# Key sums on TensorE instead of GpSimd in the first two batches of a fused attention and mixture-of-depths kernel

## The chip, the cores and the metric

The kernel runs on one core of one Trainium2 chip. TensorE (PE in the profile, with PEld for its weight loads), VectorE (DVE), ScalarE (ACT), GpSimd (POOL) and the DMA queues, issued mostly from SyncE (SP), run beside each other and are ordered by semaphores. The metric is the device time of one execution in microseconds; the time shown for the kernel before is the median of three runs.

## What is computed

Attention with RMS-normalised queries and keys, and on its output a mixture of depths: in each batch the 128 tokens with the highest score go through two layers with a residual, the other tokens are left as they are.

```python
# q, k, v: (8 batches, 12 heads, 448 tokens, 64), float32
q_n = q / sqrt(mean(q * q, -1) + 1e-6) * g_q
k_n = k / sqrt(mean(k * k, -1) + 1e-6) * g_k
p = exp(q_n @ k_n.T / 8)                      # scores, softmax
x = (p @ v) / sum(p over keys)                # (8, 448, 768)
s = x @ w_gate
top = the 128 tokens of each batch with the largest s
out = x
out[top] = x[top] + sigmoid(s[top]) * (relu(x[top] @ w1) @ w2)   # 768 -> 1024 -> 768
```

The change touches the line with `sum(p over keys)`: how the denominators are added up, and when some of the work around them is issued.

## The kernel before

**Tiling.** Four heads of one batch form a group `n`; there are 24 groups, three to a batch. The 448 keys of a group are seven tiles of 64, and one key tile of a group is a unit `u`. `scores(u)` (L292) makes four matmuls of 64x64 tiles, and ScalarE's exp (L301) turns them into a tile `p` of 128 partitions (two heads of 64 keys) by 2 x 448 queries. The ring of `p` tiles holds seven. `values(u)` (L316) multiplies `p` with `v` and accumulates a group's seven units in PSUM.

**Denominators.** `add_probs(u)` decides what becomes of a `p` tile. Normally VectorE adds the seven tiles into `sum` (L338). In the first six groups (two batches; `by_pool`) GpSimd adds tiles 0 and 1 into a buffer that once held input tokens (L332), VectorE adds tiles 2 to 5 (three additions) and then the tile of GpSimd (L342), and tile 6 goes to TensorE as it is (`sums_last`). The last group also leaves tile 6 to TensorE. `sum_keys(n)` (L372) adds over the partitions: it multiplies each term (`sum`, and a left over `p`) with `pick_pair`, a pattern of ones of 128 x 32, in four column tiles of TensorE, 224 query columns each, into the PSUM tile `den_ps`. ScalarE copies the result (L380). `invert_sums(n)` transposes it twice (L397, `denT_ps`) and takes the reciprocal on VectorE (L399, `rden`). `to_tokens(n, c)` transposes the attention output (L415, `x_ps`) and multiplies it with `rden` (L417) to give `x`.

**Gate and layers.** When a group is done, `gate(n)` (L441) multiplies `x` with the gate weights. When a batch is done, `spread` (L454), `score_rows` (L470), `count` (L486), `annotate` and `select` rank its tokens and write the chosen ones to DRAM with indirect DMAs from GpSimd (L513); `load_selected` (L531) loads them as `xe`. `mixture(g)` is a generator over the layers of a set of batches: batch 0 alone, then pairs, then single ones. It transposes `xe` (L561), runs the first layer (L590) and the second (L609, L618) and stores rows (L628). It yields after each half bank of work; what lies between two yields is called a piece.

**Order of the work.** The order is written out by a loop over sections `q` of four units in two halves. Each half issues the scores of two units and, one pair behind, the values; then `opening` takes at most one due task (`sum_keys`, `invert_sums`, `to_tokens`, `last_tokens`, `score_rows`), `run(slots)` issues what stands in the list `todo` for these two slots (loads, squares L210 and L219, the power on GpSimd L220, scaling of queries L251, gates, counts), and `piece(q)` advances the layers by one piece. `ready` holds the section from which a set of batches may begin its layers. `before_layers(q)` is true until batch 0's layers have begun; until then a bank of PSUM of their pool, `moe`, serves `denT_ps` and `x_ps`. `begin` covers the sections up to three batches' units and some more; in these, and around the third and fourth piece of a pair of batches (`slow`), the second half gets no piece. `long_next(q)` says whether the second half has a piece, in which case `invert_sums` comes right behind it in the same section.

Of the kernel before, what the change touches and what calls it, by code (L numbers as in the profile page):

```python
# [10 lines left out]
F32 = mybir.dt.float32  # L11
I32 = mybir.dt.int32
AF = mybir.ActivationFunctionType
OP = mybir.AluOpType
# [11 lines left out]
class Loads:  # L26
# [37 lines left out]
    def get(self, name, n, i=None):  # L64
        return self.tiles[name, n, i]
# [3 lines left out]
def fast(  # L69
# [21 lines left out]
    nc = tc.nc  # L91

    B, NP, _, S = loads.src["qT"].shape
    CP = 112
    NJ = S // CP
    D = 64
    NI = S // D
    H = 2 * NP
    GH = 4
    NG = H // GH  # L100
# [7 lines left out]
    n_groups = B * NG  # L108
    scale = 1.0 / math.sqrt(D)

    const = ctx.enter_context(tc.tile_pool(name="const", bufs=1))
    norm_pool = ctx.enter_context(tc.tile_pool(name="norm", bufs=2))
# [14 lines left out]
    def aux(shape, name):  # L127

        if PER * now[0] >= units:
            return ps_sc.tile(shape, F32, tag="sc", name=name)  # L130
        if spare[0]:
            return ps_moe.tile(shape, F32, tag="moe", name=name)
        return ps_aux.tile(shape, F32, tag="aux", name=name)
# [7 lines left out]
    load, get, neg_half = loads.load, loads.get, loads.neg_half  # L141

    ident = const.tile([128, 128], F32, name="ident")
# [10 lines left out]

    gg = const.tile([128, 1], F32, name="gg")

    pick_pair = const.tile([128, 32], F32, name="pick_pair")
    nc.vector.memset(pick_pair, 0.0)
    for c in range(2):
        nc.vector.memset(pick_pair[D * c : D * (c + 1), c : c + 1], 1.0)  # L160
    nc.vector.scalar_tensor_tensor(
        out=gg, in0=loads.gcol[:, 0:1], scalar=scale, in1=loads.gcol[:, 1:2], op0=OP.mult, op1=OP.mult
    )

    ps = ps_moe.tile([128, 512], F32, tag="moe", name="warm_ps")
# [116 lines left out]
    probs, sums, avs, xTs, rdens, xs = {}, {}, {}, {}, {}, {}  # L282
# [40 lines left out]

    def add_probs(u):
        n, i = divmod(u, NI)
        if i == NI - 1 and sums_last(n):
            lasts.setdefault(n, []).append(probs.pop(u))
            return
        first = 2 if by_pool(n) else 0
        if first and i == 1:  # L330
            t = first_tokens[n % 2].rearrange("p h i d -> p h (i d)")
            nc.gpsimd.tensor_tensor(out=t, in0=probs.pop(u - 1), in1=probs.pop(u), op=OP.add)  # L332
            firsts[n] = t
        elif i > first:
            begins = i == first + 1
            if begins:
                sums[n] = p_pool.tile([128, 2, S], F32, name="sum", bufs=2)
            nc.vector.tensor_tensor(  # L338
                out=sums[n], in0=probs.pop(u - 1) if begins else sums[n], in1=probs.pop(u), op=OP.add
            )  # L340
            if first and i == NI - 2:
                nc.vector.tensor_tensor(out=sums[n], in0=sums[n], in1=firsts.pop(n), op=OP.add)  # L342

    def values_out(n):
        for c in (1, 0):
# [2 lines left out]
            xTs[n, c] = t  # L348
        avs.pop(n)

    dens, lasts, firsts = {}, {}, {}

    first_tokens = [get("tok", 0, i) for i in range(2)]

    def sums_last(n):


        return n < 2 * NG or n == n_groups - 1

    def by_pool(n):  # L360

        return n < 2 * NG

    def sum_keys(n):

        ps = aux([128, 512], "den_ps")
        terms = [sums.pop(n)] + lasts.pop(n, [])
        for t in terms:
            for hh in range(2):
                for odd in range(2):  # L370
                    o = 64 * odd + 32 * hh
                    nc.tensor.matmul(  # L372
                        out=ps[o : o + 32, 0 : S // 2],
                        lhsT=pick_pair,
                        rhs=t[:, hh].rearrange("k (jj odd p) -> k odd jj p", odd=2, p=CP)[:, odd],
                        start=(t is terms[0]),
                        stop=(t is terms[-1]),
                    )
        den = norm_pool.tile([128, NJ // 2, CP], F32, name="den", bufs=1)
        nc.scalar.copy(out=den.rearrange("d j p -> d (j p)"), in_=ps[:, 0 : S // 2])  # L380
        dens[n] = den
        if n < n_groups - 1:

            q, place = now
            when = (q, place + 1) if place == 0 or long_next(q) else (q + 1, 0)
            tasks.insert(0, (when, lambda: invert_sums(n)))

    def invert_sums(n):
        den = dens.pop(n)
        shape = [128, NJ // 2, 128]  # L390
        if now[1] == 0 and PER * now[0] < units:
            pool, tag = (ps_moe, "moe") if before_layers(now[0]) else (ps_sc, "sc")
            ps = pool.tile(shape, F32, tag=tag, name="denT_ps")
        else:
            ps = aux(shape, "denT_ps")
        for jj in range(NJ // 2):
            nc.tensor.transpose(out=ps[:CP, jj, :], in_=den[:, jj, :], identity=ident)  # L397
        rden = norm_pool.tile([CP, NJ // 2, 4, 2], F32, name="rden")
        nc.vector.reciprocal(  # L399
            out=rden, in_=ps[:CP].rearrange("p jj (t r) -> p jj t r", r=32)[:, :, :, 0:2]  # L400
        )
        rdens[n] = rden.rearrange("p jj (odd hh) c -> p (jj odd) hh c", hh=2)

    def to_tokens(n, c):
        b = n // NG
        if b not in xs:
            xs[b] = x_pool.tile([CP, NJ, DX], F32, name="x")
        t = xTs.pop((n, c))
        shape = [128, NJ, 128]
        if c == 1 and not before_layers(now[0]):  # L410
            ps = ps_sc.tile(shape, F32, tag="sc", name="x_ps")
        else:
            ps = aux(shape, "x_ps")
        for j in range(NJ):
            nc.tensor.transpose(out=ps[:CP, j, :], in_=t[:, j, :], identity=ident)  # L415
        col = (n % NG * 2 + c) * 128
        nc.vector.tensor_tensor(  # L417
            out=xs[b][:, :, col : col + 128].rearrange("p j (h d) -> p j h d", d=D),
            in0=ps[:CP].rearrange("p j (h d) -> p j h d", d=D),
            in1=rdens[n][:, :, :, c, None].to_broadcast([CP, NJ, 2, D]),  # L420
            op=OP.mult,
        )
# [113 lines left out]
    group_of = {b: g for g, bs in enumerate(groups) for b in bs}  # L536
# [100 lines left out]

    HALVES = 2
    PER = 2 * HALVES
    BEGIN = 3 * NG * NI // PER + 5  # L640
    units = n_groups * NI
    todo, tasks = {}, []

    def at(slot, fn, *args):
        todo.setdefault(slot, []).append(lambda: fn(*args))
# [31 lines left out]
    for n in range(1, n_groups):  # L677
# [4 lines left out]
        if n > 1:  # L682
# [3 lines left out]
            first = max(s0 - (20 if n > 5 else 17), 0)  # L686
# [17 lines left out]

    def long_next(q):

        if before_layers(q) or q in begin:
            return False
        return 2 <= pieces[0] < pieces[1]

    def before_layers(q):
        return done == 0 and ready.get(0, q + 1) > q

    def soon():

        q, place = now
        return PER * q + 2 * place if PER * q < units else -9

    def last_tokens(n):
        to_tokens(n, 1)  # L720
        b, g = divmod(n, NG)
        s = soon()
        at(s, gate, n)
        if g < NG - 1:
            return

        at(s + 4 if s >= 0 else s, store_x, b)
        at(s + 1, spread, b)
        q, place = now

        when = (q + 1 + place // 2, 0) if b < B - 1 else (q + 1, 1)
        tasks.insert(0, (when, lambda: ranks_of(b)))

    def ranks_of(b):
        score_rows(b)
        s = soon()
        at(s, count, b, (0, 1))
        at(s + 1, count, b, (2, 3))
        at(s + 2, annotate, b)
        at(s + 2, select, b)  # L740
        at(s + 10 if s >= 0 else s + 3, load_selected, b)
        if b == B - 1:
            ready[group_of[b]] = 0
        elif b == groups[group_of[b]][-1]:
            ready[group_of[b]] = (s + 8) // PER + 1

    def run_values(upto, q):
        ended = False
# [25 lines left out]
    def short(q):  # L774

        return pieces[0] == 1

    def piece(q):

        nonlocal moe, done  # L780
        slow = range(3, 5) if q * PER < units and pieces[1] > 10 else ()
        if half == 1 and (q in begin and pieces[0] > 2 or pieces[0] in slow):
            return False
        pieces[0] += 1
        if next(moe, moe) is not moe:
            return True
        if ready.get(done, q + 1) > q:
            return False
        moe = mixture(done)
        pieces[:] = 1, 2 + 8 * len(groups[done])  # L790
        done += 1
        next(moe)
        return True


    begin = range(BEGIN)
    pieces = [0, 0]
    waiting = list(range(units))
    moe, ready, done, q = iter(()), {}, 0, 0
    while done < len(groups) or tasks:  # L800
        now[:] = q, 0
        k = PER * q
# [552 lines left out]
```

## Time and profile before

| | |
|---|---|
| median of three runs | 522.48 us (521.94 to 523.08) |
| profiled execution | 523.67 us |
| its span | 521.9 us |
| TensorE clock granted | 0.999 |
| TensorE busy | 96% of the span, 4133 matmuls and transposes |
| VectorE, ScalarE, GpSimd busy | 65%, 53%, 38% |
| DMA | 93.17 MB, mean 179 GB/s |

The profile comes from one execution, and its times are those of that execution. Its span runs from the first to the last instruction. Busy time is time in which an engine had an instruction; that says nothing yet of the path that sets the end. A group of instructions is listed by its line, engine, operation, output<-inputs and shapes, with its busy time, the mean duration of one instruction and the idle time of the engine ahead of it, with what ended the idle time. Durations of matmuls overlap, since their ends are modelled; the distance from start to start tells what one costs.

### The profile page before, as it was taken

How to read it: one execution, taken by the hardware profiler on the slowest of the kernel's cores; microseconds unless marked ns; L12 is line 12 of the kernel's file. 1: busy time of each engine (PE TensorE's matmuls, PEld its weight loads, DVE VectorE, ACT ScalarE, POOL GpSimd, SP SyncE). 2: the span in 40 equal slices, each digit the busy share in tenths (PEclk: the TensorE clock that was granted, in tenths of full speed). 3: DMA queues.
4: the chain of work that ended last, by engine and by line, in shares of the span. 5: the costliest groups of instructions: out<-in, count | busy, mean ns of one | idle time of the engine just before them, and what ended most of it. 6: DMA issues, size and time to landing. Idle time of an engine off the chain costs nothing. (4 is left out here: it accounts for less than half of the span.)

```text
span 521.9 us, 10414 instructions
## 1 busy us (share of the span) xinstructions
PE 499.3 (96%) x4133; PEld 283.1 (54%) x4133; DVE 338.0 (65%) x636; ACT 277.0 (53%) x507; POOL 198.1 (38%) x110
## 2 busy tenths in 40 slices
PE   5999898899999999999999999999999999899996
PEld 4544343365754534556654454556564464686595
DVE  4578798679867799697656775788464675440101
ACT  4887876666657667675454544764643434310010
POOL 4997768433544084435411344036110132020002
PEclk9999999999999999999999999999999999999999
DMA  8978879989864549968167373586222042031001
GB/s 298 374 239 292 292 242 334 313 233 328 274 177 131 153 142 312 261 229 261 26 201 221 107 240 111 187 264 180 80 76 68 4 148 77 1 122 47 30 32 35
DMA packets 43402, 93.17 MB, mean 179 GB/s; under 512 B 11059, under 2 KB 23348, under 8 KB 43346
## 3 DMA queue, kind: packets, MB, share of 16 engines
q1 hardware_dynamic: 39938, 86.11, 52.6%
q0 software_dynamic: 3264, 6.31, 3.4%
q8 instruction: 34, 0.56, 0.5%
q14 instruction: 22, 0.18, 0.1%
q10 hardware_dynamic: 144, 0.00, 0.0%
HBM read 74.93 MB, written 25.35 MB: 192 GB/s over the span
## 5 line engine op out<-in xcount | busy, mean ns | idle before, releaser
L301 ACT ACTIVATE p<-sc,rinv 128x448 f32<-128x448 f32 x336 | 186.5, 642 | 105.4 <-PE sc L292 79.8
L220 POOL TENSOR_TENSOR rinv<-ss,neg_half 128x14 f32<-128x14 f32 (+1 forms) x49 | 131.3, 2685 | 178.0 <-DVE ss L219 144.9
L292 PE MATMUL sc<-qT,kT 64*64 64x448 f32 x1344 | 153.2, 545 | 2.0 <-DVE x L417 1.2
L316 PE MATMUL av<-p,v 64*64 64x448 f32 x1344 | 146.8, 537 | 0.0
L338 DVE TENSOR_TENSOR sum<-sum,p 128x896 f32<-128x896 f32 x101 | 110.1, 1090 | 8.7 <-ACT p L301 2.5
L316 PEld LDWEIGHTS av<-p,v 64*64 64x64 f32 x1344 | 59.4, 133 | 67.7 <-issue 58.0
L292 PEld LDWEIGHTS sc<-qT,kT 64*64 64x64 f32 x1344 | 54.0, 132 | 70.6 <-issue 46.6
L219 DVE TENSOR_REDUCE ss<-sq 128x14 f32<-128x910 f32 (+1 forms) x49 | 52.4, 1074 | 18.7 <-ACT sq L210 18.5
L417 DVE TENSOR_TENSOR x<-x_ps,rden 112x512 f32<-112x512 f32 x48 | 32.9, 689 | 37.9 <-PE x_ps L415 34.6
L513 POOL DMA_INDIRECT selected<-x,rank x32 | 35.4, 1105 | 58.0 <-DVE x L505 50.0
L590 PE MATMUL moe_ps<-xeT,w 128*128 128x256 f32 (+1 forms) x288 | 56.0, 346 | 0.0
L609 PE MATMUL moe_ps<-w,hT 128*128 128x384 f32 x160 | 55.8, 492 | 0.0
L590 PEld LDWEIGHTS moe_ps<-xeT,w 128*128 128x128 f32 x288 | 46.2, 191 | 7.0 <-issue 2.8
L210 ACT ACTIVATE sq<-tok 128x896 f32<-128x896 f32 (+1 forms) x49 | 46.3, 952 | 6.2 <-DMA tok<-in_tok_dram 6.2
L441 DVE SCALAR_TENSOR_TENSOR prod<-x,wg 112x256 f32<-112x256 f32 x96 | 40.7, 424 | 3.1
L628 POOL DMA_INDIRECT out_dram<-xe,row x10 | 11.4, 1136 | 80.7 <-DVE xe L618 63.6
L609 PEld LDWEIGHTS moe_ps<-w,hT 128*128 128x128 f32 x160 | 28.8, 190 | 20.2 <-issue 4.3
L618 DVE SCALAR_TENSOR_TENSOR xe<-sc,xe 128x384 f32<-128x384 f32 (+1 forms) x7 | 3.9, 560 | 48.1 <-PE sc L609 48.1
L590 PE MATMUL sc<-xeT,w 128*128 128x256 f32 (+1 forms) x192 | 32.2, 328 | 0.3 <-ACT xeT L566 0.3
L609 PE MATMUL sc<-w,hT 128*128 128x384 f32 (+1 forms) x112 | 31.3, 440 | 0.0
L415 PE MATMUL x_ps<-ident,xT 128*112 128x128 f32 x192 | 28.9, 276 | 2.2 <-DVE rden L399 2.2
L590 PEld LDWEIGHTS sc<-xeT,w 128*128 128x128 f32 x192 | 28.8, 191 | 2.9 <-ACT xeT L566 0.5
(69 smaller groups left out, 316.2 us busy)
## 6 DMA issues: line engine op xcount, KB each, us to landing
tok<-in_tok_dram SPq DMA_DIRECT2D x48, 448.0 KB
qT<-in_qT_dram SPq DMA_DIRECT2D x24, 448.0 KB
kT<-in_kT_dram SPq DMA_DIRECT2D x24, 448.0 KB
v<-in_vp_dram SPq DMA_DIRECT2D x24, 448.0 KB
out_dram<-x SPq DMA_DIRECT2D x8, 1344.0 KB
bc<-rows SPq DMA_DIRECT2D x44, 224.0 KB
xe<-selected SPq DMA_DIRECT2D x8, 385.0 KB
w<-in_moe_w_dram SPq DMA_DIRECT2D x6, 512.0 KB
```

Of the source, the lines that this page charges most:

```text
L210: nc.scalar.activation(out=sq[:, h, :, 0:D], in_=t[:, h], func=AF.Square, scale=scale)
L219: nc.vector.tensor_reduce(out=ss[:, h], in_=sq[:, h], axis=AX.X, op=OP.add)
L220: nc.gpsimd.tensor_tensor(out=rinv[:, h].rearrange(flat), in0=ss[:, h].rearrange(flat), in1=neg_half.to_broadcast([128, (h.stop - h.start) ...
L292: nc.tensor.matmul(out=scs[hh][D * c : D * (c + 1), 0:S], lhsT=get("kT", n)[r, c, D * i : D * (i + 1)], rhs=get("qT", n)[r, c, :], start=True,
L301: nc.scalar.activation(out=p[:, hh], in_=scs[hh][:, 0:S], func=AF.Exp, scale=rinvs[n, 1][:, hh, i : i + 1],)
L316: nc.tensor.matmul(out=avs[n][c][D * hh : D * (hh + 1), 0:S], lhsT=get("v", n)[r, hh, i, :], rhs=probs[u][r, hh], start=(i == 0), stop=(i ...
L338: nc.vector.tensor_tensor(out=sums[n], in0=probs.pop(u - 1) if begins else sums[n], in1=probs.pop(u), op=OP.add)
L417: nc.vector.tensor_tensor(out=xs[b][:, :, col : col + 128].rearrange("p j (h d) -> p j h d", d=D), in0=ps[:CP].rearrange("p j (h d) -> p j ...
L441: nc.vector.scalar_tensor_tensor(out=prod, in0=xs[b][:, j, cols], scalar=1.0, in1=wg[:, cols], op0=OP.mult, op1=OP.mult, accum_out=gates[b ...
L513: w = nc.gpsimd.indirect_dma_start(out=t[:, :], out_offset=bass.IndirectOffsetOnAxis(ap=rank[:, j : j + 1], axis=0), in_=x[:, j, :], in_of ...
L590: nc.tensor.matmul(out=ps[:, i, :, :n], lhsT=w1[:, dc, 128 * (f0 + i) : 128 * (f0 + i + 1)], rhs=xeT[:, dc, 0:G, :n], start=(dc == 0), sto ...
L609: nc.tensor.matmul(out=ps[:n, :width], lhsT=hT[:, fc, i, :n], rhs=w2[:, fc, cols], start=(fc == 0), stop=(fc == NFC - 1),)
```

## The change

The change has two sides. In `add_probs`, `sum_keys` and `invert_sums` it alters who adds up the denominators:

- GpSimd no longer adds. In the first six groups VectorE adds tiles 0 to 4 (four additions) and tiles 5 and 6 both go to TensorE; the last group keeps one tile for TensorE.
- `pick_pair` holds two patterns of 128 x 32. Each term now takes eight matmuls of 112 columns instead of four of 224: the two values of `jj` are added into the same 112 columns of PSUM, in different rows.
- Accordingly the copy is 128 x 112, there is one transpose instead of two, and the reciprocal writes `rden` through a permuted view.

In the order of the work it alters five places: `BEGIN` is one section later; one function `single(q)` replaces the two tests for sections without a second piece, and is now also asked by `long_next`; batch 0's layers may begin one section later; the gate of group 1 is issued two slots later and that of group 22 four slots later.

```diff
-    pick_pair = const.tile([128, 32], F32, name="pick_pair")
+    pick_pair = const.tile([128, NJ // 2, 32], F32, name="pick_pair")
     nc.vector.memset(pick_pair, 0.0)
-    for c in range(2):
-        nc.vector.memset(pick_pair[D * c : D * (c + 1), c : c + 1], 1.0)
+    for jj in range(NJ // 2):
+        for c in range(2):
+            r = 2 * jj + c
+            nc.vector.memset(pick_pair[D * c : D * (c + 1), jj, r : r + 1], 1.0)
...
     def add_probs(u):
         n, i = divmod(u, NI)
-        if i == NI - 1 and sums_last(n):
+        if i >= NI - by_array(n):
             lasts.setdefault(n, []).append(probs.pop(u))
-            return
-        first = 2 if by_pool(n) else 0
-        if first and i == 1:
-            t = first_tokens[n % 2].rearrange("p h i d -> p h (i d)")
-            nc.gpsimd.tensor_tensor(out=t, in0=probs.pop(u - 1), in1=probs.pop(u), op=OP.add)
-            firsts[n] = t
-        elif i > first:
-            begins = i == first + 1
+        elif i > 0:
+            begins = i == 1
...
-            if first and i == NI - 2:
-                nc.vector.tensor_tensor(out=sums[n], in0=sums[n], in1=firsts.pop(n), op=OP.add)
...
+    def by_array(n):
+
+        return 2 if n < 2 * NG else 1 if n == n_groups - 1 else 0
...
-        for t in terms:
+        steps = [(t, jj) for t in terms for jj in range(NJ // 2)]
+        for step in steps:
+            t, jj = step
             for hh in range(2):
                 for odd in range(2):
                     o = 64 * odd + 32 * hh
                     nc.tensor.matmul(
-                        out=ps[o : o + 32, 0 : S // 2],
-                        lhsT=pick_pair,
-                        rhs=t[:, hh].rearrange("k (jj odd p) -> k odd jj p", odd=2, p=CP)[:, odd],
-                        start=(t is terms[0]),
-                        stop=(t is terms[-1]),
+                        out=ps[o : o + 32, 0:CP],
+                        lhsT=pick_pair[:, jj],
+                        rhs=t[:, hh].rearrange("k (j p) -> k j p", p=CP)[:, 2 * jj + odd],
+                        start=(step is steps[0]),
+                        stop=(step is steps[-1]),
                     )
-        den = norm_pool.tile([128, NJ // 2, CP], F32, name="den", bufs=1)
-        nc.scalar.copy(out=den.rearrange("d j p -> d (j p)"), in_=ps[:, 0 : S // 2])
+        den = norm_pool.tile([128, CP], F32, name="den", bufs=1)
+        nc.scalar.copy(out=den, in_=ps[:, 0:CP])
...
-        for jj in range(NJ // 2):
-            nc.tensor.transpose(out=ps[:CP, jj, :], in_=den[:, jj, :], identity=ident)
-        rden = norm_pool.tile([CP, NJ // 2, 4, 2], F32, name="rden")
+        nc.tensor.transpose(out=ps[:CP, :], in_=den, identity=ident)
+        rden = norm_pool.tile([CP, NJ // 2, 2, 2, 2], F32, name="rden")
...
-    BEGIN = 3 * NG * NI // PER + 5
+    BEGIN = 3 * NG * NI // PER + 6
...
-        if before_layers(q) or q in begin:
+        if before_layers(q) or single(q):
             return False
         return 2 <= pieces[0] < pieces[1]
...
-        at(s, gate, n)
+        at(s + (2 if n == 1 else 4 if n == n_groups - 2 else 0), gate, n)
...
-            ready[group_of[b]] = (s + 8) // PER + 1
+            ready[group_of[b]] = (s + 8) // PER + (1 if b else 2)
...
+    def single(q):
+
+        if q in begin:
+            return pieces[0] > 2
+        return PER * q < units and pieces[1] > 10 and pieces[0] in (3, 4)
+
     def piece(q):
 
         nonlocal moe, done
-        slow = range(3, 5) if q * PER < units and pieces[1] > 10 else ()
-        if half == 1 and (q in begin and pieces[0] > 2 or pieces[0] in slow):
+        if half == 1 and single(q):
             return False
```

More of the change, by code (lines that the diff above doesn't have):

```diff
@@ L349, in values_out @@
         avs.pop(n)
[L351 to L362, printed above, removed]
+    dens, lasts = {}, {}
+    def by_array(n):
+        return 2 if n < 2 * NG else 1 if n == n_groups - 1 else 0
     def sum_keys(n):
@@ L389, in invert_sums @@
         den = dens.pop(n)
-        shape = [128, NJ // 2, 128]
+        shape = [128, 128]
         if now[1] == 0 and PER * now[0] < units:
@@ L395, in invert_sums @@
             ps = aux(shape, "denT_ps")
-        for jj in range(NJ // 2):
-            nc.tensor.transpose(out=ps[:CP, jj, :], in_=den[:, jj, :], identity=ident)
-        rden = norm_pool.tile([CP, NJ // 2, 4, 2], F32, name="rden")
+        nc.tensor.transpose(out=ps[:CP, :], in_=den, identity=ident)
+        rden = norm_pool.tile([CP, NJ // 2, 2, 2, 2], F32, name="rden")
         nc.vector.reciprocal(
-            out=rden, in_=ps[:CP].rearrange("p jj (t r) -> p jj t r", r=32)[:, :, :, 0:2]
+            out=rden.rearrange("p jj odd hh c -> p (odd hh) jj c"),
+            in_=ps[:CP].rearrange("p (t r) -> p t r", r=32)[:, :, 0:NJ].rearrange(
+                "p t (jj c) -> p t jj c", c=2
+            ),
         )
-        rdens[n] = rden.rearrange("p jj (odd hh) c -> p (jj odd) hh c", hh=2)
+        rdens[n] = rden.rearrange("p jj odd hh c -> p (jj odd) hh c")
     def to_tokens(n, c):
```

## The prediction

> **What bounds the kernel now.** First the busy shares and the slices of the page, because the chain of waits breaks off after five short pieces here and cannot carry the bound.
>
> ```profile
> PE 499.3 (96%) x4133; PEld 283.1 (54%) x4133; DVE 338.0 (65%) x636; ACT 277.0 (53%) x507; POOL 198.1 (38%) x110
> PE   5999898899999999999999999999999999899996
> DVE  4578798679867799697656775788464675440101
> ```
>
> TensorE (PE) is busy 96% of the span, and nine tenths everywhere but at both ends and in the fifth, seventh and eighth slice, which lie in 52 to 104 us. Less PE work, or fewer PE waits, is time; other engines count only where PE waits for them. The table of stretches (stretch, its length, busy us of PE, PEld, DVE, ACT, POOL with counts, clock, DMA share, GB/s) says where:
>
> ```profile
> 52.00:78.00 26.00, 23.35 (x250) 10.07 (x246) 22.18 (x38) 20.77 (x39) 17.50 (x6) 1.00 0.80 265
> 78.00:104.00 26.00, 21.65 (x230) 10.21 (x222) 19.80 (x37) 16.42 (x31) 17.19 (x9) 1.00 1.04 325
> 104.00:200.00 96.00, 94.95 (x879) 51.13 (x876) 79.30 (x147) 62.70 (x114) 41.04 (x20) 1.00 0.70 211
> ```
>
> From 52 to 104 us PE stands still for 7.0 us (2.65 + 4.35), beside a VectorE (DVE) that is 85% and 76% busy. From 104 to 200 it stands still for 1.05 us. The clock is full, so no gain or loss comes from it. Next the PE timeline, for each idle stretch and its releaser (start, length, instruction, [idle before]):
>
> ```profile
> 57.13 0.58 PE L372 MATMUL den_ps<-sum,pick_pair 128*32 128x224 f32 x8 [1.60 <-DVE sum L342]
> 101.82 0.55 PE L561 MATMUL moe_ps<-ident,xe 128*128 128x128 f32 x3 [2.17 <-DMA xe<-selected]
> 191.52 0.58 PE L372 MATMUL den_ps<-sum,pick_pair 128*32 128x224 f32 x8 [1.05 <-DVE sum L338]
> 231.76 0.43 PE L397 MATMUL denT_ps<-ident,den 128*112 128x128 f32 x2 [0.49 <-ACT den L380]
> 450.18 0.59 PE L372 MATMUL den_ps<-sum,pick_pair 128*32 128x224 f32 x8 [1.35 <-DVE row L573]
> ```
>
> Idle time there understates a stall, since a matmul's end is modelled. I take start to start minus the normal spacing: 1.67 us at 57 (den of group 2), 1.12 at 74 (den 3), 2.27 at 84 (x_ps of group 3, for rden), 2.33 at 101.8 (the xe load), 1.12 at 191 (den 10), 0.56 at 231 and 0.54 at 348 (denT right behind den), 1.42 at 450 (den 23). Last, the groups by shape (busy, mean ns of one, idle before):
>
> ```profile
> L372 PE MATMUL den_ps<-sum,pick_pair 128*32 128x224 f32 x192 | 14.1, 365 | 5.3 <-DVE sum L342 2.7 <-DVE row L573 1.3 <-DVE sum L338 1.0
> L372 PE MATMUL den_ps<-p,pick_pair 128*32 128x224 f32 x56 | 3.9, 352 | 0.0
> L397 PE MATMUL denT_ps<-ident,den 128*112 128x128 f32 x48 | 10.0, 290 | 1.0 <-ACT den L380 1.0
> L470 PE MATMUL row_ps<-ident,gate 112*112 112x112 f32 x32 | 4.6, 266 | 0.0
> L332 POOL TENSOR_TENSOR tok<-p 128x896 f32<-128x896 f32 x6 | 13.5, 2249 | 0.0
> ```
>
> **TensorE: the sums.** 31 terms (24 sums and seven p tiles) of four matmuls leave 248 records, so a float32 matmul is two passes, and each pass of the four column tiles is a set. Starts of two sets lie 189.5 ns apart at 224 columns; from the first start to the next other instruction a group of one term takes 515 ns, of two 894. The change gives 37 terms of eight matmuls, four sets of 112 columns each. No set of four tiles at 112 columns is in this trace. The nearest row is L470, 112 columns on one tile: 95.5 ns start to start, also half of 189.5. I take 96, and 233 ns around the intervals: 25 and 20 at the first set, and the 282 behind the last start less 94 for 112 columns. One term: 3 × 96 + 233 = 521 (+6 ns, 17 times). Three terms: 11 × 96 + 233 = 1289 (+395 ns, six times). The last group: 7 × 96 + 233 = 905 (+11). Sum +2.48 us, all but 0.11 in the opening. The upper end of a set is 117 ns: L262's 64-column matmuls, each with its load, start every 29.2 ns, four of them 117. Over 17 × 3 + 6 × 11 + 7 = 124 intervals that is +2.6 us. [...]
>
> [...]
>
> **TensorE: one denT.** 24 transposes of 128 columns go, 109 ns each by the spacing in the pair: −2.62 us, of which 2.07 in the 19 groups behind the opening. The copy L380 (345 ns) and rden shrink or stay; ACT at 53% hides them.
>
> **The opening, 26 to 104 us.** Six GpSimd adds go (13.5 us). DVE keeps four adds per group: three and the join become four. But they no longer wait for GpSimd, nor run beside it: the add at 33.17 took 2.98 us and the join at 71.59 took 2.80, both beside an L332, against 1.09 otherwise. The catch is order: the fourth add now stands with the others, and in groups 2 and 3 the four (three in 1 and 4) are ahead of the previous group's rden on DVE. Behind rden waits x_ps of c = 1 on PE, as denT and x_ps share a bank, and behind that PE's scores. Before this is already seen:
>
> ```profile
> 80.86 2.29 DVE L338 TENSOR_TENSOR sum<-sum,p 128x896 f32<-128x896 f32 x2
> 83.25 1.09 DVE L342 TENSOR_TENSOR sum<-sum,tok 128x896 f32<-128x896 f32 x1
> 84.26 0.25 DVE L399 RECIPROCAL rden<-denT_ps 112x16 f32<-112x16 f32 x1
> 84.61 0.69 DVE L417 TENSOR_TENSOR x<-x_ps,rden 112x512 f32<-112x512 f32 x1
> ```
>
> I replayed DVE's queue by hand with 1.19 us per dependent add. rden of group 1 goes from 49.15 to 50.6: PE +1.47 us. Den 2's stall is gone, but rden 2 goes from 65.42 to 67.3, so PE is 1.9 late there; den 3's stall gone leaves +1.18; rden 3 at 84.7 for 84.26 leaves PE +0.45 at 86 us, since the stall of 2.27 there absorbs it. Den 4 costs its 0.395: +0.84. Batch 0's layers begin one section later, so the xe transposes follow den 5 and denT 5. The load lands at 101.8, and PE has work until about then: −2.33, while 0.71 us of layer work is only moved. Net at 104 us: −0.8 us, with the den and denT terms inside. If no stall moved on, it would be −7.4 + 2.4 − 0.5 = −5.5; if the xe load still stopped PE, +1.5.
>
> **Behind the opening.** (a) At 191 us the shift of batch 0's layers by one section puts a half layer of L609 (about 2.6 us of PE) ahead of den 10, and DVE's sum is ready: −1.12; ends 0 and −1.12. (b) Batches whose denT came right behind den get it a section later (14 and 20), with a half section between: −1.10; ends 0 and −1.10. What is late next is the x behind it; DVE at 200 to 300 us has room. (c) Group 22's gate, four operations of 0.42 us and their reads, 1.76 us, stood on DVE ahead of the last sum; it now follows the last rden: −1.42. It delays batch 7's choice only if its row counting waits for it: its last xe load was issued at 472.3 and needed at 494.6, and that slack hides it. The gate of group 1, two slots later, frees DVE ahead of the adds; inside the replay. SP's instruction order is unchanged, GpSimd's only loses the adds; the p ring of seven loses tiles 0 and 1 sooner and holds tile 5 until den, with at most six in use.
>
> **Sum:** −0.8 − 2.07 + 0.11 − 1.12 − 1.10 − 1.42 = −6.4 us. The profiled execution took 523.67 us (span 521.9, 1.8 around it), so 517.3 there; against the median of 522.48, **516.1 us**.
>
> **Rivals.**
> - *A, as above*: 516.1, own range 514.0 to 518.5, chance 0.48.
> - *B, the opening's waits just vanish*: the exps or score banks, not rden, release PE, and the DVE tail is hidden. For it: DVE loses two overlong adds (3.6 us together) and all waiting for GpSimd. Against: rden at 84.26 already ended a PE wait with four adds ahead. −5.5 for −0.8: 511.4, chance 0.14.
> - *C, the gaps come back*: den 10 still waits for DVE's sum (DVE is 83% busy from 104 to 200), the moved denT finds its x late, and the opening ends at +0.2. 516.1 + 1.1 + 1.1 + 1.0 = 519.3, chance 0.26. For it: every gap of this kernel so far ended at DVE.
> - *D, slower*: L372 is bound by issue. [...] It decides from a set of 96 + 6.4/0.124 = 148 ns on. [...] Chance 0.12.
> - That the change doesn't do what it says: the instruction order shows 592 den records, 24 denT, no L332; excluded.
>
> **Numbers.** 0.2% is 1.04 us, about what a measurement can tell from no change. The range reaches from B to the upper part of C, 511.0 to 521.5, and leaves out D and some tail of B and C. Faster: A, B and most of C, 0.79; same: the rest of C, 0.08; slower: D and a little, 0.13.
>
> **What would show it.** Den sets 96 ns apart in the profile after; three-term groups at about 1.29 us; rden of group 2 at 67 us; no stall at 57 and 74, but one of about 2 us at the x_ps behind rden 1 and rden 2; no wait on xe near 102; no wait for DVE at den 23. A set above 148 ns, or 200 to 450 us longer than before, would make the forecast wrong.

## The result and the profile after

The changed kernel took 519.85 us (median of six executions, 519.74 to 520.38), beside 522.62 us for the kernel before in the same set: a ratio of 0.995, 95% interval 0.9938 to 0.9963. The forecast was 516.1. The time lies in the range that was forecast and the gain has its sign, but it is 2.8 us and not 6.4.

That number did not come again. The same program was run in three further sets of executions (e5, whose profile is called the rerun below, e9 and e13), and took 516.21 (515.75 to 516.32), 516.12 (515.61 to 518.25) and 515.86 us (515.50 to 516.05), beside 523.21, 522.96 and 522.49 for the kernel before: ratios of 0.9871 (0.9841 to 0.9901), 0.9852 (0.9818 to 0.9885) and 0.987 (0.985 to 0.9889). So there are two questions: where the 3.7 us between the first set and the others lie, and whether the steps of the forecast hold in the others.

First the page of the first set's profile, in the rows that were shown of before (the counts are of records, and a float32 matmul leaves two: 592 for the 296 of the sums):

```profile
PE 502.0 (97%) x4453; PEld 288.0 (56%) x4453; DVE 333.5 (64%) x638; ACT 274.6 (53%) x507; POOL 181.1 (35%) x104
PE   5999988999999999999999999999999999999996
DVE  4657779689867888788656765788564675530101
```

GpSimd is down by 17 us, 13.5 of them the additions. Of TensorE's slices below nine, which were the fifth, seventh and eighth, the sixth and seventh are left. Then the same stretches (stretch, length, busy PE, PEld, DVE, ACT, POOL, clock, DMA share, GB/s):

```profile
52.00:78.00 26.00, 24.30 (x317) 11.29 (x321) 19.42 (x40) 20.18 (x38) 12.49 (x4) 1.00 0.80 276
78.00:104.00 26.00, 24.21 (x306) 11.38 (x302) 21.24 (x43) 17.72 (x33) 14.65 (x8) 1.00 1.02 330
104.00:200.00 96.00, 95.88 (x903) 50.91 (x891) 77.40 (x142) 61.33 (x114) 40.00 (x20) 1.00 0.75 228
```

From 52 to 104 us TensorE now idles 3.5 us, where it idled 7.0. From 104 to 200 the idle time nearly vanished, and yet this is where the time was lost: a TensorE that issues slowly still counts as busy (the 24 records of the values from 192.30 us are one busy stretch of 3.86 us, in the rerun, from 190.71, one of 2.44). It shows only when starts are set against those of another profile. The timeline of ScalarE in the first set's profile (start, length, instruction, [idle before]) has the place:

```profile
187.84 0.98 ACT L341 COPY xT<-av 128x448 f32<-128x448 f32 x2
194.46 0.25 ACT L369 COPY den<-den_ps 128x112 f32<-128x112 f32 x1 [5.65 <-PE av L318]
194.61 0.96 ACT L212 ACTIVATE sq<-tok 128x896 f32<-128x896 f32 x1
```

and in the rerun:

```profile
186.25 0.98 ACT L341 COPY xT<-av 128x448 f32<-128x448 f32 x2
189.32 0.25 ACT L369 COPY den<-den_ps 128x112 f32<-128x112 f32 x1 [2.08 <-PE den_ps L361]
189.47 0.96 ACT L212 ACTIVATE sq<-tok 128x896 f32<-128x896 f32 x1
```

The copy of group 10's sums waits for the sums. In the rerun it starts 0.09 us behind their end; in the first set's profile the sums ended at 190.81 and the copy started 3.65 us later. ScalarE did not sit on sums that it knew to be ready. TensorE's instructions count up one semaphore (804 of them in the changed kernel), and the trace has the times of these steps. In all 16 profiles this copy starts 0.02 us behind a step. In the other 15 the step comes within 0.1 us of the sums' end (at 189.30 for 189.23 in the rerun). Here the steps of the last two matmuls of the sums, of four scores and of one of the values, seven in all, come between 193.71 and 194.77, the second of them, for which the copy waited, at 194.44. So the row is right to name TensorE as the releaser, though not the values, which are only the nearest instruction to that step. TensorE's weight loads of the same moment:

```profile
192.30 0.15 PEld L318 LDWEIGHTS av<-p,v 64*64 64x64 f32 x4 [0.22 <-issue]
192.69 0.13 PEld L318 LDWEIGHTS av<-p,v 64*64 64x64 f32 x1 [0.24 <-issue]
193.04 0.17 PEld L318 LDWEIGHTS av<-p,v 64*64 64x64 f32 x2 [0.21 <-issue]
193.72 0.13 PEld L318 LDWEIGHTS av<-p,v 64*64 64x64 f32 x1 [0.51 <-issue]
```

Loads that otherwise come four at a time come singly, with nothing shown that they wait for. Whether the matmuls themselves were late or only the word of them can't be told, since a matmul's end is modelled in the profile. The delay near 90 us has the same look: a copy of ScalarE started at 89.32, 0.02 us behind a step of TensorE, and no step had come since 86.56. The exps (the instructions that make `p`) give the sum: setting the start of each exp of this profile against the rerun's, the program is 0.65 us late from the first one on (the first tokens' squares started 0.31 us later, when their load had landed, and TensorE's first small matmuls then took 2.83 us for 2.37), 1.27 after 91 us, 1.59 after 136, 3.74 at 198 and 4.69 from 205 us to the end. The two spans differ by the same 4.7 (518.7 and 514.0).

### The profile page after: what moved, and what is told of

Its sections match the earlier page's. It is cut to its first block, busy times and chain, and to the rows that moved or that the text cites. A ratio compares the mean times of both kernels' runs of the same rounds, so it can differ in the third digit from the quotient of the medians.

```text
span 518.7 us, 11063 instructions
## 1 busy us (share of the span) xinstructions
PE 502.0 (97%) x4453; PEld 288.0 (56%) x4453; DVE 333.5 (64%) x638; ACT 274.6 (53%) x507; POOL 181.1 (35%) x104
## 5 line engine op out<-in xcount | busy, mean ns | idle before, releaser
L294 PE MATMUL sc<-qT,kT 64*64 64x448 f32 x1344 | 155.0, 545 | 1.8 <-DVE x L408 0.9
L318 PE MATMUL av<-p,v 64*64 64x448 f32 x1344 | 149.9, 537 | 0.2
L334 DVE TENSOR_TENSOR sum<-sum,p 128x896 f32<-128x896 f32 x107 | 116.6, 1090 | 8.7 <-ACT p L303 2.4
L504 POOL DMA_INDIRECT selected<-x,rank x32 | 32.4, 1014 | 55.3 <-DVE x L496 47.3
```

Of the source, the lines that this page charges most:

```text
L294: nc.tensor.matmul(out=scs[hh][D * c : D * (c + 1), 0:S], lhsT=get("kT", n)[r, c, D * i : D * (i + 1)], rhs=get("qT", n)[r, c, :], start=True,
L318: nc.tensor.matmul(out=avs[n][c][D * hh : D * (hh + 1), 0:S], lhsT=get("v", n)[r, hh, i, :], rhs=probs[u][r, hh], start=(i == 0), stop=(i ...
L334: nc.vector.tensor_tensor(out=sums[n], in0=probs.pop(u - 1) if begins else sums[n], in1=probs.pop(u), op=OP.add)
L504: w = nc.gpsimd.indirect_dma_start(out=t[:, :], out_offset=bass.IndirectOffsetOnAxis(ap=rank[:, j : j + 1], axis=0), in_=x[:, j, :], in_of ...
```

## The experiments

Each of e1 to e4, e5 to e8, e9 to e12 and e13 with e14 is one set of executions, and the kernel before ran beside each: 522.79, 523.21, 522.96 and 522.49 us.

**The two halves of the change.** e1 takes the sums alone:

```diff
-    BEGIN = 3 * NG * NI // PER + 6
+    BEGIN = 3 * NG * NI // PER + 5
...
-        if before_layers(q) or single(q):
+        if before_layers(q) or q in begin:
...
-        at(s + (2 if n == 1 else 4 if n == n_groups - 2 else 0), gate, n)
+        at(s, gate, n)
...
-            ready[group_of[b]] = (s + 8) // PER + (1 if b else 2)
+            ready[group_of[b]] = (s + 8) // PER + 1
```

(and the old test in `piece`). e2 is the other half: the kernel before with these lines the other way round.

> Only the sums of the change: no GpSimd addition, two tiles of the first six groups and narrow matmuls on TensorE, one transpose. The order of the work stays as before. Theory A (the parts are worth what the prediction gave them, and what was lost lies in the new order): the transposes give 2.6 us back, the narrow matmuls take 2.5, the opening loses its waits on the joined sum but waits for the reciprocal behind four additions, so about 1 us faster than before (521.6). Theory B (the order is what pays and the sums cost): no faster than before or slower, 522.6 to 524.

> Only the order of the change: one section later for batch 0's layers, the test for sections without a second piece, the two later gates. GpSimd adds as before, the matmuls stay 224 columns wide, two transposes. Theory A: the waits before the sums of group 10 and 23, the two at the transposed sums and the one for the loaded tokens go, about 3 to 4 us, so 519 to 520, as fast as the whole change. Theory B (most of the order's gain is given back in a new stall at 193 us, which belongs to the order): 520.5 to 521.5.

The sums alone took 520.70 us (519.66 to 525.89, twelve executions; ratio 0.9977, 0.9951 to 1.0003), the order alone 517.48 (516.85 to 520.46; ratio 0.9904, 0.9871 to 0.9938). That is 2.1 and 5.3 us by the medians, together 7.4, which is about what the reruns of the whole change gained (6.6 to 7.0). Theory B falls: the order pays, and no stall at 193 us came with it (its copy of group 10's sums starts 0.07 us behind them). The sums don't cost; that they pay is likely by their profile, but their interval just reaches no gain (1.0003). The order pays more than was put down to it. In its profile the wait before the sums of group 2, which the forecast gave to GpSimd's going, is gone although GpSimd still adds:

```profile
54.32 0.93 PE L316 MATMUL av<-p,v 64*64 64x448 f32 x8
55.18 0.59 PE L372 MATMUL den_ps<-sum,pick_pair 128*32 128x224 f32 x8
```

The gate of group 1, two slots later, left VectorE free for the additions: in the kernel before, its products start at 50.91 us, ahead of them, and in e2 at 54.84, behind them. In e1's profile the wait is gone as well: either half of the change removes these 1.67 us, and the whole has them once. So the halves add up only roughly: 7.4 less 1.67 is about a microsecond short of what the whole gained, within what the medians of e1 and e2 can tell.

**Is the stall at 193 us part of the program?** e3 puts back group 22's gate, e4 shifts ScalarE's instructions by 64 small copies, e8 repeats 64 matmuls of the sums; e5, e9 and e13 are the changed kernel itself.

```diff
-        at(s + (2 if n == 1 else 4 if n == n_groups - 2 else 0), gate, n)
+        at(s + (2 if n == 1 else 0), gate, n)
```

is e3,

```diff
             run(slots)
+            if half == 1 and 12 <= q < 28:
+                for _ in range(4):
+                    nc.scalar.copy(out=pad, in_=neg_half)
```

e4 and

```diff
-        for step in steps:
+        for step in (steps if 6 <= n < 10 else []) + steps:
```

e8.

> The changed kernel with the gate of group 22 at its old place. Until about 430 us all engines have the same instructions as the changed kernel, so it also repeats the stall of 2.4 us at 193 to 199 us, where ScalarE stood idle for 5.65 us. If that stall belongs to the program, this profile shows it again, to within some tenths; if it was an accident of one execution, it is gone. The gate: the wait of 1.42 us before the sums of the last group is back, so 1.4 us slower than the changed kernel (521.3); if the last group's sums are hidden otherwise, the same time (519.9).

> The changed kernel with 64 small copies of one column added on ScalarE, four at the end of each section from the 12th to the 27th (60 to 180 us or so), which shift ScalarE's later instructions by 64 places. Theory A (the stall at 193 us is ScalarE waiting for its instructions to be fetched): ScalarE's idle time of 5.65 us moves to another place or goes, and the kernel becomes up to 2 us faster. Theory B (the stall follows from what ScalarE and TensorE wait for there): it stays at den of group 10, and the time stays at 519.9 or grows by some tenths for the copies.

> The changed kernel once more, unchanged, beside others. The kernel with only the gate of group 22 put back ran 2.5 us faster than it (517.4), and its profile, with the same instructions until 430 us, lacked the stall at 193 us and smaller ones at 90, 127 and 134 us, 3.9 us in all, and had the wait of 1.4 us at the last sums. Theory P (the stalls belong to this program as it is laid out, in every execution): 519.9 again, with ScalarE idle for 5 us or more before the den copy of group 10. Theory C (they belonged to the place or the time of those executions): they are gone, and the time is 517.4 - 1.4 = 516.0.

> The changed kernel in which the sums of groups 6 to 9 are computed twice on TensorE, the first time for nothing: 64 matmuls more, four times 0.38 us. It shifts TensorE's instructions behind 120 us by 128 places. Theory P: the stalls at 193 us depend on where instructions lie, so they go or move: 517.5. Theory C: 516.0 + 1.5 = 517.5 as well, and the rerun beside it at 516.0; if the stall follows from the work itself, 519.9 + 1.5 = 521.4.

> The changed kernel, unchanged, for a third time and in another set of executions. Theory C (the 3.9 us of stalls belonged to the first set of executions alone): 516.0 to 516.5 again, no stall at den of group 10. Theory M (the program has two ways to run, a fast and a slower one, and each set of executions falls into one): either 516.2 or 519.9 in all executions of this set, and if 519.9, ScalarE idle for 5 us or more before the den copy of group 10.

> The changed kernel, unchanged, in a further set of executions. Two sets of reruns gave 516.2 and 516.1, the first set 519.9 in all six of its executions. Theory C (something of that first set alone): 516.0 to 516.5, no idle of ScalarE ahead of the den copy of group 10. Theory M (each set falls into one of two ways of running): 519.9 can come again, and then the second profile tells whether the stall stands at the same instruction.

e3 took 517.37 us, e4 517.52, e8 517.26. None of their profiles has the stall; the copy of group 10's sums follows 2.1 us of idle time in each, as in the reruns. e3 has the changed kernel's instructions until 430 us and lacked it, so it isn't the order of the work. e4, which could have spoken for ScalarE's instruction stream, can't any more, since the unchanged program lacks it too. What is shown is that the program alone doesn't make the stall, since three further sets of the same program lack it (theory C). One execution of the first set was profiled; that the other five had the stall too is inferred from their times, all six within 0.7 us. Its cause stays open. The profiles exclude the clock (1.00 in both from 104 to 200 us), and the volume of DMA was no larger (64.2% and 66.8% of the engines' time on the large queue from 180 to 210 us). Two transfers of 8 KB on the queue that the page calls instruction ran within 1 us of the sums' end, at 190.71 and 191.74, but the reruns have such a pair at the same place, without the stall. One mark sets both profiles of the first set apart from the 14 later ones: steps of semaphores are missing from their traces (20 of VectorE's 504, 19 of ScalarE's 506 and 5 of TensorE's 804 in the changed kernel's; 8, 11 and 5 in that of the kernel before), and none from the others. Whether that goes with the stall isn't shown. Nor is the chip excluded: the record names chip 14 for e1 to e4, 9 for e5 to e12, 4 for e13 and e14, and none for the first set.

e3 also measures its own edit. The wait before the last sums is back:

```profile
442.19 0.49 PE L552 MATMUL xeT_ps<-ident,xe 128*128 128x128 f32 x3
444.02 0.59 PE L361 MATMUL den_ps<-sum,pick_pair 128*32 128x112 f32 x16 [1.34 <-DVE sum L334]
```

Start to start this is 1.42 us over normal, as in the kernel before; its time stands 1.2 us above that of the unchanged program, which ran in another set. e8 costs 1.50 us in its profile from the last doubled sum to the end and 1.05 by the medians, for a forecast of 4 x 0.38.

**The other edits of the order.** e6 has the old tests for sections without a second piece, e7 batch 0's layers at their old section:

```diff
-    BEGIN = 3 * NG * NI // PER + 6
+    BEGIN = 3 * NG * NI // PER + 5
...
-        if before_layers(q) or single(q):
+        if before_layers(q) or q in begin:
```

is e6 (with the old test in `piece`), and e7 is

```diff
-            ready[group_of[b]] = (s + 8) // PER + (1 if b else 2)
+            ready[group_of[b]] = (s + 8) // PER + 1
```

> The changed kernel with the old tests for sections without a second piece and the old BEGIN. Prediction's steps: the two waits at the transposed sums (0.56 and 0.54 us) come back, so 1.1 us slower than the changed kernel without its stalls (517.1). If the piece ahead of the sums of group 10 depends on BEGIN too, the wait of 1.1 us there also comes back: 518.2. Theory P of the rerun: a program of another layout, so the stalls may be gone or elsewhere, and the time is 517 to 518.2; theory C: the same times, and the rerun is at 516.0.

> The changed kernel with batch 0's layers at their old section. Prediction's steps: TensorE waits again for the loaded tokens near 100 us (1.3 us in the profile of the kernel with the sums alone), and since the layers are a piece ahead again, the half layer no longer stands before the sums of group 10, whose wait of 1.1 us is back: 2.4 us slower than the changed kernel without its stalls, 518.4. If the two gains belong to other edits: 516.0 to 516.5.

e6 took 517.39 us, 1.2 more than the rerun beside it. The two waits at the transposed sums are back; the first is

```profile
228.26 0.32 PE L385 MATMUL denT_ps<-ident,den 128*112 128x128 f32 x1 [0.37 <-ACT den L369]
```

They are shorter than before (0.35 us each for 0.56 and 0.54), as the copy that they wait for is (256 ns for 348). The wait before the sums of group 10 is not back, so it hangs on batch 0's section and not on BEGIN. e7 took 518.08 (517.12 to 521.63), 1.9 more. Its profile shows which of the two waits it was:

```profile
99.92 0.55 PE L552 MATMUL moe_ps<-ident,xe 128*128 128x128 f32 x3
...
189.28 0.59 PE L361 MATMUL den_ps<-sum,pick_pair 128*32 128x112 f32 x16 [1.07 <-DVE sum L334]
```

The wait before group 10's sums came back (1.14 us), and one of 1.04 us at the scores behind it (1880 ns for 842), but none for the loaded tokens: here they had landed when TensorE came.

**The first profile of before, once more.**

> The kernel before, unchanged, for a second profile of it. Theory C: its first profile was free of such stalls, so the waits of TensorE are the same in kind and size (1.67, 1.12, 2.27, 2.33, 1.12, 0.56, 0.54, 1.42 us), and the time is 522.5 to 523.2. If its first profile had such stalls too, this one is faster, by 1 us or more.

522.88 us, the same as the kernel before beside it (ratio 0.9993, 0.9966 to 1.0020). The waits came again to some hundredths (den of group 2: 2135 ns in both; x_ps: 2460 and 2454), except one: the wait of 2.33 us for the loaded tokens is absent. In this execution TensorE was 1.7 us later by then and lost nothing by it. That wait depends on when a load lands. The two profiled executions took 523.67 us with it and 522.70 without.

**What is left in the opening.** e11 issues up to two of the additions behind the reciprocal, e14 does so in the whole kernel, e12 gives TensorE a third tile.

```diff
-            run_values(k + 2 * half - 1, q)
+            run_values(k + 2 * half - 1, q, half == 1 and len(dens) > 0 and before_layers(q))
         opening(q, 0)
+        while late:
+            add_probs(late.pop(0))
...
-            add_probs(u)
+            if hold:
+                late.append(u)
+            else:
+                add_probs(u)
```

is e11; e14 leaves out its last condition. e12 is the changed kernel with

```diff
-        return 2 if n < 2 * NG else 1 if n == n_groups - 1 else 0
+        return 3 if n < 2 * NG else 1 if n == n_groups - 1 else 0
```

> The changed kernel in which, until batch 0's layers begin, the additions of a section's second half are issued behind the transposed sums and the first x of the group before (while sums wait to be inverted), so that VectorE has at most two additions, not four, ahead of the reciprocal. Theory of the prediction (what the opening gains is held down by the reciprocal behind the additions): the waits of x_ps at 50, 65 and 83 us (0.84, 1.78 and 1.56 us in the rerun) fall to 0 to 0.6 each, and 2 to 3.5 us are gained against the changed kernel: 513 to 514. Rival (the additions that come later only make the next sums late): the waits move to the sums, and the time stays at 516.

> The changed kernel in which TensorE sums three tiles of the first six groups instead of two: 8 narrow matmuls more per group, 4 x 96 = 0.38 us, six times 2.3 us of TensorE, and one addition of 1.09 us less on VectorE. Theory of the prediction: the waits of x_ps at 65 and 83 us shorten by 1.2 us each, the one at 50 us by 0.8, so 3.2 saved for 2.3 spent: 515 to 515.5. If TensorE's time alone counts: 516.2 + 2.3 = 518.5.

> The changed kernel with the late additions in the whole kernel, not only until batch 0's layers begin. In the run before, 3.9 us were gained until 96 us, and 2.2 us lost again at 106 and 109 us, where additions once more stood ahead of the reciprocal. Theory of the reciprocal: that loss goes too, so 512 to 512.5. Rival (later x or sums are late instead, as VectorE is 80% busy there): 514 to 516.

In e11 the three waits of x_ps are gone, and TensorE is 3.9 us ahead of the rerun at 86 us, as the theory said. Then it meets the next reciprocal, and the `x` behind it, in the section in which batch 0's layers have begun and nothing is held back:

```profile
107.05 1.05 PE L294 MATMUL sc<-qT,kT 64*64 64x448 f32 x8 [0.24 <-DVE rden L387]
109.45 0.60 PE L294 MATMUL sc<-qT,kT 64*64 64x448 f32 x3 [1.35 <-DVE row L564]
```

2.2 us are lost there and 1.6 remain. By time it is 514.99 us (512.38 to 517.41; ratio 0.9839, 0.9796 to 0.9882) beside 516.12 for the changed kernel: the best of all versions by its median, but the intervals overlap. e14 removes that loss and pays it elsewhere: with its later start taken out it is 3.6 us ahead at 107 us, 1.7 at 200 and 0.1 at the end, and takes 515.93 us. The rival was right there: TensorE's losses stand at scores that an `x` of VectorE releases, at 129, 149, 217 and 335 us, and VectorE is busy for 78 of the 96 us from 104 to 200. e12 removes the waits at 65 and 83 us and shortens the one at 50 to 0.46 (649 ns for 188), pays 2.3 us for it (sums of 1671 ns for 1288, six times), and ends at 515.98: no gain, a little less than was expected. Until 110 us it is 1.3 us ahead of the rerun; 1.2 of that go at the same scores as in e11, in a wait of 0.92 us at 111.67.

## Why the prediction was right or wrong

**The bound, the sums and the transposes: right.** The groups by shape of the first set's profile (busy, mean ns of one, idle before):

```profile
L361 PE MATMUL den_ps<-sum,pick_pair 128*32 128x112 f32 x384 | 14.2, 265 | 0.4 <-DVE x L408 0.4
L385 PE MATMUL denT_ps<-ident,den 128*112 128x128 f32 x24 | 7.4, 307 | 0.0
L361 PE MATMUL den_ps<-p,pick_pair 128*32 128x112 f32 x208 | 6.3, 259 | 0.0
```

Sets start 96 ns apart (forecast 96). A group of one term takes 521 ns to the next instruction (521), of three 1288 (1289), the last 905 (905). The sums cost 2.46 us more on TensorE, transposes give 2.81 back for a forecast 2.62. No run shows a matmul of the sums that is bound by issue, on which the slower case (D, 0.12 of the 0.13 for slower) rested. In this profile the four tiles of a set start 6 to 7 ns apart, and sets of 112 columns 96 ns where those of 224 started 189.5 apart; within a group's sums no neighbouring sets start more than 120 ns apart (the first two of each), beside the 148 from which D would have decided. So that case fell.

**The opening: mechanism right, sum 0.5 us too cautious.** The replay had the reciprocals of groups 1 to 3 behind the additions, and x_ps behind them. In the rerun:

```profile
63.64 3.49 DVE L334 TENSOR_TENSOR sum<-sum,p 128x896 f32<-128x896 f32 x3
67.05 0.25 DVE L387 RECIPROCAL rden<-denT_ps 112x16 f32<-112x16 f32 x1
```

and TensorE, at the same moment:

```profile
65.06 0.60 PE L406 MATMUL x_ps<-ident,xT 128*112 128x128 f32 x4
67.35 0.65 PE L406 MATMUL x_ps<-ident,xT 128*112 128x128 f32 x4 [1.69 <-DVE rden L387]
```

67.05 for a forecast of 67.3. With the rerun's earlier start of 0.2 us taken out, TensorE was 1.4 us later than before at unit 20 (forecast 1.47), 1.8 at 28 (1.9), 0.8 at 32 (1.18), level at 36 (0.45), and 2.0 ahead at 44 (1.5, the net 0.8 with the 0.7 of moved work). At 44 the sum itself had a slip. It set the 0.71 us of moved work against the gain, though the wait of 2.33 goes whether that work moves or not, and it left out the 0.395 that den 5 costs too, less 0.11 for its transpose. Put right, the net is -1.2 us, and TensorE would have been 1.9 ahead. The waits behind the reciprocals of groups 1 and 2 are 0.84 and 1.78 us, where about 2 were named for each, so the first was less than half of that; the one of 1.56 at 83 us is what is left of 2.27. The case in which the waits just vanish (B) is thereby refuted too.

**Behind the opening: right in the reruns, with one gain not seen.** The waits at the sums of group 10, at the transposed sums of groups 12 and 18 (at 231 and 348 us; the prediction numbers them 14 and 20) and at the last sums are gone: 1.12, 1.10 and 1.42, each as put. e3, e6 and e7 bring them back one by one, at their sizes or shorter. Not forecast was that the scores at 202 us, which wait for an x of VectorE, lose 0.9 of their 1.36 us of waiting; e7 ties this to batch 0's section as well. The forecast's 6.4 with the opening's 0.5, these 0.9, the start's 0.2 and 0.2 more from the transposes make 8.2, beside 8.1 us measured at the last matmul and 7.9 at the span's end between the two profiles. By the medians the gain is 6.6 to 7.0, as the profiled execution of before was 1.2 us above its median. That the reruns' 516.2 met the forecast's 516.1 so closely is therefore in part luck: gains that were not forecast stand against a price for the loaded tokens that not every execution pays.

**What failed.** Against the time of the first set it is the step "The copy L380 (345 ns) and rden shrink or stay; ACT at 53% hides them", at group 10. It took the copy as free once the sums are made, and looked only at how busy ScalarE is. The 1.12 us of (a) were gained, since TensorE did not wait before these sums. But TensorE's semaphore told of them 3.6 us after their end; ScalarE, idle for 5.65 us, made the copy and the exps behind it as late, and the next scores waited for these exps:

```profile
196.14 0.19 PEld L294 LDWEIGHTS sc<-qT,kT 64*64 64x64 f32 x2 [0.77 <-ACT p L303]
```

With a later `x` behind them TensorE lost 3.1 us until 205 us against the rerun, more than the step had gained. The other 0.65 at the start, 0.65 near 90 and 0.3 near 135 us are of the same set. Why the semaphore's steps came late stays open. A forecast from one profile of before could not have it, as no copy of sums in before starts more than 0.3 us behind their end, and three further sets of the changed kernel don't show it at group 10 either. Case C, which named about this time (519.3), is not what happened, and its number is luck: it had the waits for VectorE come back, and none of them did. (Its ground, that every gap of this kernel ended at DVE, was also a wrong reading: among the prediction's own lines one ends at a DMA and one at ScalarE.)

One attribution was wrong though its number came out: the 2.33 us at the loaded tokens were not a fixed price that the later section saves. They came and went between two profiles of the same kernel before, and the kernel with batch 0's layers at the old section (e7) didn't pay them.

## What to carry to other kernels

Price the narrow form of a matmul by the column rate of a row in the same profile, with the start-to-start distance and not the mean duration; here sets came 96 ns apart at 112 columns and 189.5 at 224, and three different bursts came out within 1 ns. When work is taken from an engine that made another wait, ask what stands ahead of the next small instruction that TensorE needs: here a reciprocal of 0.25 us behind three or four additions held TensorE for 4.2 us in three waits, and moving additions behind it only helped where VectorE had room later (3.9 us gained by 86 us in e11; in e14, with VectorE busy for 78 of the 96 us from 104 to 200, 0.1 was left of 3.6). When an engine starts late on work that seems ready, look at when the semaphore told it so, before blaming the engine. And before a shortfall of half a per cent is explained, run the same program in another set of executions: here the set mattered more (3.7 us) than any edit but the order as a whole.

## What was unexpected of the hardware

TensorE's clock dropped right behind a wait in some executions. In the second profile of before, after a wait of 2.18 us (the stretch of six us, then the timeline):

```profile
84.00:90.00 6.00, 5.09 (x36) 2.12 (x37) 5.76 (x14) 2.24 (x5) 5.36 (x4) 0.72 1.06 287
```

```profile
84.91 0.67 PE L415 MATMUL x_ps<-ident,xT 128*112 128x128 f32 x4 [2.18 <-DVE rden L399]
85.51 3.27 PE L292 MATMUL sc<-qT,kT 64*64 64x448 f32 x16
```

Four sets of scores started some 747 ns apart for the usual 376, and cost 1.5 us more. The granted clock is 0.72 in this stretch, and 0.50 from 85.5 to 88.8 us. The changed kernel had the same at 69 us in e9's profile, behind its wait of 1.78 us (granted 0.74 from 66 to 72 us, and 0.50 from 68.9 to 72.2), and that execution took 518.25 us for a median of 516.12. So in that profile of before the stretch behind the wait cost 1.5 us on top of the wait's 2.18. The half clock came behind waits of 1.8 and 2.2 us within busy work, in one execution and not in another of the same kernel: in the first profile of before the granted clock is 1.00 from 84 to 90 us, behind a wait of 2.19 us, and in the changed kernel's first profile 1.00 from 66 to 72, behind one of 1.70 (idle time; 1.69 in the rerun, where 1.78 is start to start). 747 ns for 376 fits the granted 0.50; what brings it on isn't shown.
